# Output accumulators as two PSUM tiles, and the last unit in halves, in a convolution and rational-activation kernel

## The chip, the cores and the metric

The kernel runs on one core of one Trainium2 chip. The metric is the device time of one execution in microseconds (us), which is that of its one core. A core has five engines with a queue each: TensorE (PE in the profile; PEld is its weight load), VectorE (DVE), ScalarE (ACT), GpSimd (POOL) and SyncE (SP, which here only issues DMAs). Matmuls write to PSUM; ScalarE and VectorE read it.

## The reference, cut to what matters

```python
def _attn_ref(x, weight):                       # x (8, 4096, 192), weight (8, 7)
    w = softmax(weight, axis=-1)                # exp(weight - max) / (sum + 1e-9)
    x_pad = concatenate([zeros((B, 6, D)), x], axis=1)
    x_unf = x_pad[:, arange(S)[:, None] + arange(7)[None, :], :].reshape(B, S, 7, 8, 24)
    return einsum('hk,bskhg->bshg', w, x_unf).reshape(B, S, D)

def _moe_ref(x, w_in, w_out, a, b):             # x (32768, 192), w_in (192, 2048), w_out (2048, 192)
    h = x @ w_in
    P = a[0] + a[1]*h + a[2]*h**2 + a[3]*h**3
    Q = 1.0 + abs(b[0])*abs(h) + abs(b[1])*h**2
    g = P / (Q + 1e-6)
    return g @ w_out
```

A causal 7-tap convolution with softmaxed taps goes into two matrix products with a rational function between them.

## The kernel before, in words

The 32768 tokens are cut into 64 chunks of 512 (`NCH`, `CH`), and the 2048 hidden features into 8 units of 256 (`UPC`), so there are 512 units (`NU`); unit k is feature block k mod 8 of chunk k div 8. For each unit:

- TensorE makes the first product into a PSUM tile `hp` of 128 x 1024 (`gemm1`, line 512, ten matmuls, task `g1`); two such tiles exist.
- ScalarE makes five passes over 128 x 1024: `A` (line 583) and `S` into tile `t` (line 579), both from `hp`; `B` in place on `A` (line 586); `L`, a logarithm, into `l` (line 593); `Y`, an exponential, into a PSUM tile `y` (line 597).
- VectorE makes four passes, all recorded at the helper `stt` (line 305): `V` (`t<-t,hp`), `m` (`g<-t,y`), `e` (`A<-A,y`) and `g` (`g<-A,g`), the last of which finishes the unit.
- TensorE makes the second product (`gemm2`, line 521, task `g2`): eight matmuls add the unit to the chunk's output accumulator `op`, first the four of token pair 0, then the four of pair 1. The trace shows two PE records for each of these matmuls, so 16 for a unit.

The accumulator is one PSUM tile of 4 x 256 columns, from a pool with one buffer (`ps_o`). After a chunk's eighth unit ScalarE copies it out in two parts (`out_evac`, line 530, tasks `("O", c, 0)` and `("O", c, 1)`, tile `ob`), and SyncE sends each part to memory. The next chunk's accumulator takes the same buffer.

GpSimd and its accumulating DMAs do the convolution of a later chunk (tile `acc`), paced by VectorE's `g` passes.

The order on each engine is written out by a planner (`plan`): each task has an engine, an assumed cost, dependencies and a rank, and a simulated clock puts them into a list. The TensorE order is fixed by hand: `g1` of unit k, then `g2` of unit k-3 (`LAG`). `plan` already treats the two parts of the output separately: the first `g2` of a chunk depends, for pair p, on `("O", c - 1, p)` alone. The waits that the chip obeys, however, come from the tiles that the recorded instructions read and write.

The kernel has two bodies for two kinds of coefficients; the inputs here take the one called `fast`.

Of the kernel before, what the change touches and what calls it, by code (L numbers as in the profile page):

```python
# [10 lines left out]
F32 = mybir.dt.float32  # L11
# [5 lines left out]
ALU = mybir.AluOpType  # L17
# [3 lines left out]
NB, S, D = 8, 4096, 192  # L21
# [3 lines left out]
P = 128  # L25
CH = 512
NCH = T // CH
CPB = S // CH
FT = DF // P
UPC = FT // 2  # L30
NU = NCH * UPC
# [6 lines left out]
C_Q = 1.0 + EPS_Q  # L38
F64_MIN = float(np.uint32(0x38000000).view(np.float32))
LAG = 3  # L40
NG_BUF = LAG + 3
# [24 lines left out]
def plan(fast):  # L66
# [3 lines left out]
    def add(name, engine, cost, deps, rank, release=0):  # L70
        locked = (engine == "POOL" and name[0] != "a") or (engine == "DVE" and name[0] in LOCKED)
        tasks[name] = (engine, cost, [d for d in deps if d], rank, release, locked)
# [23 lines left out]
    pe = [("c", 0, 1), ("c", 0, 0)]  # L96
# [6 lines left out]
    for c in range(NCH):  # L103
        for k in range(KT if c > 1 else 0):
            rank = 8 * window(c, k)
            add(("x", c, k), "POOL", COST["x"], [after_unit(c, k), ("a", c, k - NTMP) if k > NTMP else None,
                ("x", c, k - 1) if k else ("x", c - 1, KT - 1) if c > 2 else ("t", 2)]
                + ([("l", c - 2, 1)] if k == 0 and c > 3 else []), rank)
            if k:
                add(("a", c, k), "POOL", COST["a"], [("x", c, k), ("a", c, k - 1) if k > 1 else ("x", c, 0)], rank)  # L110
        if c > 1:
            old = [("g1", (c - 2) * UPC + UPC - 1)]
            add(("h", c), "POOL", COST["h"], [("a", c, KT - 1), after_unit(c, KT + 2)] + old, -100)
        for half in range(2):
            if c > 1:
                add(("l", c, half), "POOL", COST["l"], [("h", c), ("l", c, 0) if half else None, after_unit(c, KT + 3 + half)], -100)
                continue
            rank = -48 - 8 * half + 8 * c * SECOND
            add(("xh", c, half), "ACT", COST["xh"] * (1 + 0.4 * half), [("c", c, half)], rank)
            add(("xl", c, half), "DVE", COST["xl"] * (1 + 0.4 * half), [("xh", c, half)], rank)  # L120
        for pair in range(2):
            add(("O", c, pair), "ACT", COST["O"], [("g2", c * UPC + UPC - 1, pair)],
                8 * ((c + 1) * UPC) + (19 if pair else -30))
    if not fast:
        add(("k", 0), "DVE", COST["k"], [], -50, BODY_AT)
# [1 line left out]
    for k in range(NU):  # L127
        c, i = divmod(k, UPC)

        def old(n, *names):  # L130
            return [(name, k - n) for name in names] if k >= n else []

        add(("g1", k), "PE", COST["g1"], [("l" if c > 1 else "xl", c, 0), ("l" if c > 1 else "xl", c, 1)] + old(2, "V", "A", "S")
            + ([wdep("i", i)] if c == 0 else []), 0)
        add(("S", k), "ACT", COST["S"], [("g1", k), ("kr", 0)] + old(4, "m"), 8 * k + 1)
        add(("A", k), "ACT", COST["A"], [("g1", k), ("kr", 0)] + old(4, "g"), 8 * k)
        if fast:
            add(("B", k), "ACT", COST["B"], [("A", k)], 8 * k + 0.5)
            add(("V", k), "DVE", COST["V"], [("S", k)], 8 * k + 2)
            add(("L", k), "ACT", COST["L"], [("B", k)] + old(2, "Y"), 8 * k + 3)  # L140
        else:
            add(("B", k), "ACT", COST["B"], [("g1", k), ("kr", 0)] + old(2, "Y"), 8 * k + 2)
            add(("Q", k), "POOL", COST["Q"], [("A", k), ("B", k)], 8 * k + 3)
            add(("U", k), "DVE", COST["U"], [("S", k)], 8 * k + 1)
            add(("V", k), "DVE", COST["V"], [("U", k)], 8 * k + 2)
            add(("L", k), "ACT", COST["L"], [("Q", k)], 8 * k + 3)
        add(("Y", k), "ACT", COST["Y"], [("L", k)] + old(1, "e")
            + ([("xl", 1, 0), ("xl", 1, 1)] if k == SECOND else []), 8 * k + 4)
        add(("m", k), "DVE", COST["m"], [("V", k), ("Y", k)] + old(NG_BUF, "G"), 8 * k + 5)
        add(("e", k), "DVE", COST["e"], [("Y", k)], 8 * k + 6)  # L150
        add(("g", k), "DVE", COST["g"], [("m", k), ("e", k)], 8 * k + 7)
        for pair in range(2):
            add(("g2", k, pair), "PE", COST["g2"], [("g", k)] + ([wdep("o", i)] if c == 0 else [])
                + ([("O", c - 1, pair)] if c and i == 0 else []), 0)
    for k in range(NU + LAG):
        if k == SECOND + SECOND_LAG:
            pe += [("c", 1, 1), ("c", 1, 0)]
        if k < NU:
            pe.append(("g1", k))
        if k >= LAG:  # L160
            pe += [("g2", k - LAG, 0), ("g2", k - LAG, 1)]

    after, need, ready = {}, {}, {}
# [41 lines left out]
def kernel(  # L205
# [13 lines left out]
    nc = tc.nc  # L219
# [84 lines left out]
    def stt(out_, a, s, b, op0, op1):  # L304
        return nc.vector.scalar_tensor_tensor(out=out_, in0=a, scalar=s, in1=b, op0=op0, op1=op1)  # L305
# [71 lines left out]
    def body(fast):  # L377
# [133 lines left out]
                for n, (w, part, x) in enumerate(terms):  # L511
                    nc.tensor.matmul(H[k][:, j, :], lhsT=w[:, i, part, j, :], rhs=x, start=(n == 0), stop=(n == 4))  # L512

        def gemm2(k, pair):
            c, i = divmod(k, UPC)
            if i == 0 and pair == 0:
                O[c] = ps_o.tile([P, 4, 256], F32, name="op")
            for j in range(2):
                f = 2 * i + j
                for t in (2 * pair, 2 * pair + 1):  # L520
                    nc.tensor.matmul(O[c][:, t, 0:D], lhsT=G[k][:, j, t * P:t * P + P], rhs=wo_t[:, f, :],  # L521
                                     start=(f == 0 and t % 2 == 0), stop=(f == FT - 1 and t % 2 == 1))
            if pair == 1:
                del G[k]

        def out_evac(c, pair):
            ob = opool.tile([P, 2, D], F32, name="ob")
            o = O[c][:, 2 * pair:2 * pair + 2, 0:D]
            if fast:
                nc.scalar.activation(out=ob, in_=o, func=AF.Copy, scale=K["rO"])  # L530
            else:
                nc.scalar.copy(out=ob, in_=o)
            nc.sync.dma_start(out=out_v[c, pair], in_=ob)
            if pair == 1:
                del O[c]

        def flat(t):
            return t.rearrange("p a b -> p (a b)")
# [28 lines left out]
                K["r" + name] = nc.scalar.alloc_register(f"r_{name}_{fast}")  # L567
                nc.scalar.reg_load(K["r" + name], x[0:1].bitcast(I32))

        def unit(kind, k):  # L570
            h = flat(H[k]) if k in H else None
            s = st.get(k, {})
            if kind == "k":
                coefficients()
            elif kind == "kr":
                registers()
            elif kind == "S":
                if fast:
                    nc.scalar.activation(out=work_tile(k, "t"), in_=h, func=AF.Square, scale=K["rt"], bias=1.0)  # L579
                else:  # L580
                    nc.scalar.activation(out=work_tile(k, "t"), in_=h, func=AF.Identity, scale=K["rt"], bias=K["c2"])
            elif kind == "A":
                nc.scalar.activation(out=work_tile(k, "A"), in_=h, func=AF.Abs, scale=K["rA"])  # L583
            elif kind == "B":
                if fast:
                    nc.scalar.activation(out=s["A"], in_=s["A"], func=AF.Square, bias=1.0)  # L586
                else:
                    nc.scalar.activation(out=work_tile(k, "l"), in_=h, func=AF.Square, scale=K["rB"])
            elif kind == "Q":
                nc.gpsimd.tensor_tensor(out=s["A"], in0=s["A"], in1=s["l"], op=ALU.add)  # L590
            elif kind == "L":
                if fast:
                    nc.scalar.activation(out=work_tile(k, "l"), in_=s["A"], func=AF.Ln, scale=K["rL"], bias=1.0)  # L593
                else:
                    nc.scalar.activation(out=s["l"], in_=s["A"], func=AF.Ln, bias=C_Q)
            elif kind == "Y":
                nc.scalar.activation(out=work_tile(k, "y"), in_=s["l"], func=AF.Exp, scale=-1.0)  # L597
            elif kind == "U":
                nc.vector.tensor_tensor(out=s["t"], in0=s["t"], in1=h, op=ALU.mult)
            elif kind == "V":  # L600
                stt(s["t"], s["t"], K["c1"], h, ALU.add, ALU.mult)
            elif kind == "m":
                G[k] = gpool.tile([P, 2, CH], F32, name="g")
                stt(flat(G[k]), s["t"], K["c0"], s["y"], ALU.add, ALU.mult)
            elif kind == "e":
                stt(s["A"], s["A"], K["d"] if fast else C_Q, s["y"], ALU.add, ALU.mult)
            elif kind == "g":
                last_step[k] = stt(flat(G[k]), s["A"], K["d2"] if fast else 2.0, flat(G[k]), ALU.subtract, ALU.mult).ins
                del st[k], H[k]

        with tc.manual_schedule(engines={E.PE, E.Activation, E.DVE, E.Pool}):
            for kind, *which in plan(fast):
# [67 lines left out]
```

## Time and profile before

| what | value |
|---|---|
| median of 3 runs | 2666.54 us (2665.88 to 2666.84) |
| the profiled execution | 2666.89 us |
| its span in the trace | 2664.70 us, so 2.19 us lie outside |
| mean granted TensorE clock | 0.995 of full speed |
| busy share of PE, DVE, ACT, POOL | 95%, 94%, 95%, 46% |

A row of the timeline gives start and duration in us, engine, line, operation and tiles; in brackets stands the idle time before it and what ended it. Durations overlap: an engine may start the next instruction before the one before has ended, so the pace is read from the distance of starts. In the waits, each row says which group waited for which, with the total in us, the count and the longest.

### The profile page before, as it was taken

To read this page: it belongs to the slowest core of one execution; us is meant where nothing else is said; L and a number is where in the kernel's file an instruction comes from. 1 tells how busy PE (TensorE), PEld (TensorE's weight loads), DVE (VectorE), ACT (ScalarE), POOL (GpSimd) and SP (SyncE) were. 2 spreads that over 40 slices of the span, in tenths; PEclk is the share of its full clock that TensorE was granted. 3 is DMA by queue.
4 is the path that set the end of the run, shared out by engine and by line. 5 is a ranking of instruction groups with operands and counts; after the bars stand their busy time and mean duration, and the time that the engine had idled before them with its cause. 6 is when DMAs were issued, how large, how long until landed. Compare 5 with 4: busy or idle time off the path is not lost.

```text
span 2664.7 us, 35994 instructions
## 1 busy us (share of the span) xinstructions
PE 2534.2 (95%) x13528; PEld 2299.1 (86%) x13528; DVE 2516.9 (94%) x2160; ACT 2539.2 (95%) x2739; POOL 1235.7 (46%) x1452
## 2 busy tenths in 40 slices
PE   5999999999999999999999999999999999999998
PEld 4888888888888888888888888888888888888887
DVE  8999999999999999999999999999999999999998
ACT  7999999999999999999999999999999999999997
POOL 4454454544544444545445445454454444454530
PEclk8999999999999999999999999999999999999999
DMA  5445444445444444444544544444444444444430
GB/s 156 99 98 107 101 100 99 97 104 104 92 105 101 99 103 102 98 105 93 107 96 97 107 102 99 99 97 103 104 94 104 102 98 103 102 98 104 94 76 14
DMA packets 101721, 263.96 MB, mean 99 GB/s; under 512 B 9760, under 2 KB 44832, under 8 KB 101536
## 3 DMA queue, kind: packets, MB, share of 16 engines
q0 software_dynamic: 53568, 195.06, 38.4%
q1 hardware_dynamic: 47664, 66.04, 8.5%
q8 instruction: 108, 1.77, 0.3%
q14 instruction: 77, 0.63, 0.1%
q10 hardware_dynamic: 304, 0.46, 0.1%
HBM read 41.32 MB, written 25.17 MB: 25 GB/s over the span
## 4 chain that ended last, share of the span: by engine, by line
PE 87%; ACT 8%; DVE 2%; issue 2%; DMA 0%; POOL 0%; SPq 0%; DVEq 0%; ACTq 0%
PE op L521 50%; PE hp L512 38%; ACT l L593 2%; ACT A L586 2%; ACT ob L530 2%; ACT t L579 1%; DVE g L305 1%; DVE A L305 0%; DVE t L305 0%; ACT y L597 0%; DVE wo_t L399 0%; ACT ad L385 0%; ACT A L583 0%; PE y L434 0%; DMA wb_t<-in_wband 0%
## 5 line engine op out<-in xcount | busy, mean ns | idle before, releaser
L521 PE MATMUL op<-wo_t,g 128*128 128x192 f32 x8192 | 1424.4, 327 | 100.9 <-ACT ob L530 90.3
L521 PEld LDWEIGHTS op<-wo_t,g 128*128 128x128 f32 x8192 | 1355.6, 190 | 163.8 <-ACT ob L530 116.4
L512 PE MATMUL hp<-xh,wh_t 128*128 128x512 f32 x2048 | 872.5, 426 | 15.3 <-DVE t L305 10.6
L305 DVE SCALAR_TENSOR_TENSOR g<-t,cf,y 128x1024 f32<-128x1024 f32 x512 | 655.2, 1280 | 95.6 <-ACT y L597 78.9
L305 DVE SCALAR_TENSOR_TENSOR t<-t,cf,hp 128x1024 f32<-128x1024 f32 x512 | 653.9, 1277 | 33.8 <-ACT t L579 33.8
L305 DVE SCALAR_TENSOR_TENSOR g<-A,cf,g 128x1024 f32<-128x1024 f32 x512 | 657.0, 1283 | 1.2
L305 DVE SCALAR_TENSOR_TENSOR A<-A,cf,y 128x1024 f32<-128x1024 f32 x512 | 654.0, 1277 | 0.0
L512 PE MATMUL hp<-xh,wl_t 128*128 128x512 f32 x2048 | 633.5, 391 | 0.0
L583 ACT ACTIVATE A<-hp 128x1024 f32<-128x1024 f32 x512 | 522.1, 1020 | 49.5 <-PE hp L512 33.3
L593 ACT ACTIVATE l<-A 128x1024 f32<-128x1024 f32 x512 | 542.6, 1060 | 6.2
L586 ACT ACTIVATE A<-A 128x1024 f32<-128x1024 f32 x512 | 541.6, 1058 | 0.0
L597 ACT ACTIVATE y<-l 128x1024 f32<-128x1024 f32 x512 | 525.6, 1027 | 4.2 <-DVE xl L499 0.2
L579 ACT ACTIVATE t<-hp 128x1024 f32<-128x1024 f32 x512 | 522.0, 1020 | 0.0
L447 POOL TENSOR_SCALAR tmp<-xt,wt_t,zero 128x512 f32<-128x512 f32 x496 | 377.5, 767 | 209.3 <-DVE g L305 202.6
L512 PEld LDWEIGHTS hp<-xh,wl_t 128*128 128x128 f32 x2048 | 386.1, 189 | 86.7 <-DVE wl_t L407 0.2
L512 PEld LDWEIGHTS hp<-xh,wh_t 128*128 128x128 f32 x2048 | 387.1, 189 | 80.0 <-DVE t L305 7.3
L453 POOL DMA_DIRECT2D acc<-tmp x248 | 214.9, 867 | 414.0 <-DMA acc<-xs 369.1
L512 PE MATMUL hp<-xl,wh_t 128*128 128x512 f32 x1024 | 403.4, 394 | 0.0
L447 POOL TENSOR_SCALAR xs<-xt,wt_t,zero 128x512 f32<-128x512 f32 x248 | 188.7, 767 | 205.8 <-DVE g L305 205.8
L512 PEld LDWEIGHTS hp<-xl,wh_t 128*128 128x128 f32 x1024 | 194.2, 190 | 20.4 <-DVE xl L499 0.3
L473 POOL TENSOR_SCALAR xh<-acc,one,zero 128x1024 fp32r<-128x1024 f32 x62 | 74.2, 1198 | 251.0 <-DVE g L305 245.6
L453 POOL DMA_DIRECT2D acc<-xs x124 | 109.4, 882 | 61.3 <-DMA acc<-tmp 43.1
(57 smaller groups left out, 424.3 us busy)
## 6 DMA issues: line engine op xcount, KB each, us to landing
acc<-tmp POOLq DMA_DIRECT2D x248, 512.0 KB, 4.5
acc<-xs POOLq DMA_DIRECT2D x124, 512.0 KB, 5.2
xt<-in_xt SPq DMA_DIRECT2D x62, 518.0 KB, 4.0
out<-ob SPq DMA_DIRECT2D x128, 192.0 KB, 2.6
raw<-in_w_in SPq DMA_DIRECT2D x8, 512.0 KB, 5.7
raw<-in_w_out SPq DMA_DIRECT2D x8, 384.0 KB, 4.1
xs<-in_xa ACTq DMA_DIRECT2D x1, 324.0 KB, 4.7
xs<-in_xa SPq DMA_DIRECT2D x1, 324.0 KB, 6.5
```

The costliest lines, as they stand in the source:

```text
L305: return nc.vector.scalar_tensor_tensor(out=out_, in0=a, scalar=s, in1=b, op0=op0, op1=op1)
L447: ins = nc.gpsimd.tensor_scalar(to[:, n * CH:n * CH + CH], of[:, n * XA + k:n * XA + k + CH], wt_t[:, n, k:k + 1], zero, ALU.mult, ALU.add)
L453: nc.gpsimd.dma_start(out=CP[c], in_=TMP.pop((c, k)), accum_op=ALU.add)
L473: ins = nc.gpsimd.tensor_scalar(X[c][0].rearrange("p a b -> p (a b)"), CP[c], one, zero, ALU.mult, ALU.add)
L512: nc.tensor.matmul(H[k][:, j, :], lhsT=w[:, i, part, j, :], rhs=x, start=(n == 0), stop=(n == 4))
L521: nc.tensor.matmul(O[c][:, t, 0:D], lhsT=G[k][:, j, t * P:t * P + P], rhs=wo_t[:, f, :], start=(f == 0 and t % 2 == 0), stop=(f == FT - 1 ...
L530: nc.scalar.activation(out=ob, in_=o, func=AF.Copy, scale=K["rO"])
L579: nc.scalar.activation(out=work_tile(k, "t"), in_=h, func=AF.Square, scale=K["rt"], bias=1.0)
L583: nc.scalar.activation(out=work_tile(k, "A"), in_=h, func=AF.Abs, scale=K["rA"])
L586: nc.scalar.activation(out=s["A"], in_=s["A"], func=AF.Square, bias=1.0)
L593: nc.scalar.activation(out=work_tile(k, "l"), in_=s["A"], func=AF.Ln, scale=K["rL"], bias=1.0)
L597: nc.scalar.activation(out=work_tile(k, "y"), in_=s["l"], func=AF.Exp, scale=-1.0)
```

## The change

The accumulator becomes two tiles, `op0` and `op1`, of 2 x 256 columns each, one for each token pair, each with a buffer of its own; `gemm2` allocates the pair's tile when its chunk begins, and `out_evac` reads the pair's tile and drops it. In the last unit (k = 511) the passes `m`, `e` and `g` run on halves of 512 columns each, with half-size matmul groups behind each half, and the last chunk's output copies depend on the second half.

```diff
@@ -119,7 +119,7 @@
             add(("xh", c, half), "ACT", COST["xh"] * (1 + 0.4 * half), [("c", c, half)], rank)
             add(("xl", c, half), "DVE", COST["xl"] * (1 + 0.4 * half), [("xh", c, half)], rank)
         for pair in range(2):
-            add(("O", c, pair), "ACT", COST["O"], [("g2", c * UPC + UPC - 1, pair)],
+            add(("O", c, pair), "ACT", COST["O"], [("g2", c * UPC + UPC - 1, pair) + ((1,) if c == NCH - 1 else ())],
                 8 * ((c + 1) * UPC) + (19 if pair else -30))
     if not fast:
         add(("k", 0), "DVE", COST["k"], [], -50, BODY_AT)
@@ -146,6 +146,14 @@
             add(("L", k), "ACT", COST["L"], [("Q", k)], 8 * k + 3)
         add(("Y", k), "ACT", COST["Y"], [("L", k)] + old(1, "e")
             + ([("xl", 1, 0), ("xl", 1, 1)] if k == SECOND else []), 8 * k + 4)
+        if k == NU - 1:
+            for j in range(2):
+                add(("m", k, j), "DVE", 670, [("V", k), ("Y", k)] + old(NG_BUF, "G"), 8 * k + 4 * j)
+                add(("e", k, j), "DVE", 670, [("Y", k)], 8 * k + 4 * j + 1)
+                add(("g", k, j), "DVE", 670, [("m", k, j), ("e", k, j)], 8 * k + 4 * j + 2)
+                for pair in range(2):
+                    add(("g2", k, pair, j), "PE", COST["g2"] / 2, [("g", k, j)], 0)
+            continue
         add(("m", k), "DVE", COST["m"], [("V", k), ("Y", k)] + old(NG_BUF, "G"), 8 * k + 5)
         add(("e", k), "DVE", COST["e"], [("Y", k)], 8 * k + 6)
         add(("g", k), "DVE", COST["g"], [("m", k), ("e", k)], 8 * k + 7)
@@ -157,7 +165,9 @@
             pe += [("c", 1, 1), ("c", 1, 0)]
         if k < NU:
             pe.append(("g1", k))
-        if k >= LAG:
+        if k == NU + LAG - 1:
+            pe += [("g2", k - LAG, pair, j) for j in range(2) for pair in range(2)]
+        elif k >= LAG:
             pe += [("g2", k - LAG, 0), ("g2", k - LAG, 1)]
 
     after, need, ready = {}, {}, {}
@@ -511,28 +521,26 @@
                 for n, (w, part, x) in enumerate(terms):
                     nc.tensor.matmul(H[k][:, j, :], lhsT=w[:, i, part, j, :], rhs=x, start=(n == 0), stop=(n == 4))
 
-        def gemm2(k, pair):
+        def gemm2(k, pair, only=None):
             c, i = divmod(k, UPC)
-            if i == 0 and pair == 0:
-                O[c] = ps_o.tile([P, 4, 256], F32, name="op")
-            for j in range(2):
+            if i == 0:
+                O[c, pair] = ps_o.tile([P, 2, 256], F32, name=f"op{pair}")
+            for j in range(2) if only is None else [only]:
                 f = 2 * i + j
                 for t in (2 * pair, 2 * pair + 1):
-                    nc.tensor.matmul(O[c][:, t, 0:D], lhsT=G[k][:, j, t * P:t * P + P], rhs=wo_t[:, f, :],
+                    nc.tensor.matmul(O[c, pair][:, t % 2, 0:D], lhsT=G[k][:, j, t * P:t * P + P], rhs=wo_t[:, f, :],
                                      start=(f == 0 and t % 2 == 0), stop=(f == FT - 1 and t % 2 == 1))
-            if pair == 1:
+            if pair == 1 and only != 0:
                 del G[k]
 
         def out_evac(c, pair):
             ob = opool.tile([P, 2, D], F32, name="ob")
-            o = O[c][:, 2 * pair:2 * pair + 2, 0:D]
+            o = O.pop((c, pair))[:, :, 0:D]
             if fast:
                 nc.scalar.activation(out=ob, in_=o, func=AF.Copy, scale=K["rO"])
             else:
                 nc.scalar.copy(out=ob, in_=o)
             nc.sync.dma_start(out=out_v[c, pair], in_=ob)
-            if pair == 1:
-                del O[c]
 
         def flat(t):
             return t.rearrange("p a b -> p (a b)")
@@ -567,8 +575,9 @@
                 K["r" + name] = nc.scalar.alloc_register(f"r_{name}_{fast}")
                 nc.scalar.reg_load(K["r" + name], x[0:1].bitcast(I32))
 
-        def unit(kind, k):
+        def unit(kind, k, *half):
             h = flat(H[k]) if k in H else None
+            part = slice(CH * half[0], CH * half[0] + CH) if half else slice(0, W)
             s = st.get(k, {})
             if kind == "k":
                 coefficients()
@@ -600,13 +609,16 @@
             elif kind == "V":
                 stt(s["t"], s["t"], K["c1"], h, ALU.add, ALU.mult)
             elif kind == "m":
-                G[k] = gpool.tile([P, 2, CH], F32, name="g")
-                stt(flat(G[k]), s["t"], K["c0"], s["y"], ALU.add, ALU.mult)
+                if half in ((), (0,)):
+                    G[k] = gpool.tile([P, 2, CH], F32, name="g")
+                stt(flat(G[k])[:, part], s["t"][:, part], K["c0"], s["y"][:, part], ALU.add, ALU.mult)
             elif kind == "e":
-                stt(s["A"], s["A"], K["d"] if fast else C_Q, s["y"], ALU.add, ALU.mult)
+                stt(s["A"][:, part], s["A"][:, part], K["d"] if fast else C_Q, s["y"][:, part], ALU.add, ALU.mult)
             elif kind == "g":
-                last_step[k] = stt(flat(G[k]), s["A"], K["d2"] if fast else 2.0, flat(G[k]), ALU.subtract, ALU.mult).ins
-                del st[k], H[k]
+                g = flat(G[k])[:, part]
+                last_step[k] = stt(g, s["A"][:, part], K["d2"] if fast else 2.0, g, ALU.subtract, ALU.mult).ins
+                if half != (0,):
+                    del st[k], H[k]
 
         with tc.manual_schedule(engines={E.PE, E.Activation, E.DVE, E.Pool}):
             for kind, *which in plan(fast):
```

On all engines the instructions stand in the order of before, except in the last unit; what differs elsewhere is which tile is named and which waits are set. On TensorE at a chunk boundary in the middle of the kernel, before: the last first-product matmuls of a unit and then the new chunk's first second-product matmuls (in brackets the engines waited for; 49 is the number of the fast body's semaphores).

```order
L512 MATMUL hp_13357<-xl_13096,wh_t_182 128x512
L512 MATMUL hp_13357<-xh_13095,wh_t_182 128x512
L512 MATMUL hp_13357<-xh_13095,wl_t_183 128x512 x2
L521 MATMUL op_13374<-wo_t_184,g_13315 128x192 [waits DVE_49,PE_49,Activation_49]
L521 MATMUL op_13374<-wo_t_184,g_13315 128x192 x7
L512 MATMUL hp_13396<-xh_13095,wh_t_182 128x512 [waits DVE_49]
```

The same place on TensorE in the changed kernel:

```order
L522 MATMUL hp_13400<-xl_13139,wh_t_182 128x512
L522 MATMUL hp_13400<-xh_13138,wh_t_182 128x512
L522 MATMUL hp_13400<-xh_13138,wl_t_183 128x512 x2
L531 MATMUL op0_13417<-wo_t_184,g_13358 128x192 [waits DVE_49,Activation_49]
L531 MATMUL op0_13417<-wo_t_184,g_13358 128x192 x3
L531 MATMUL op1_13428<-wo_t_184,g_13358 128x192 [waits Activation_49]
L531 MATMUL op1_13428<-wo_t_184,g_13358 128x192 x3
L522 MATMUL hp_13440<-xh_13138,wh_t_182 128x512 [waits DVE_49]
```

The one wait for ScalarE ahead of eight matmuls has become one ahead of the first four and another ahead of the last four. On ScalarE at the same boundary, before (`ob<-op` is the output copy; the DMAHW wait is for an old transfer out of the buffer `ob`):

```order
L597 ACTIVATE y_13341<-l_13330 128x1024 [waits DVE_49,Activation_49]
L530 ACTIVATE ob_13347<-op_13076 128x384 [waits DMAHW6_49,PE_49]
L586 ACTIVATE A_13337<-A_13337 128x1024 [waits Activation_49]
L579 ACTIVATE t_13368<-hp_13317 128x1024
L593 ACTIVATE l_13371<-A_13337 128x1024 [waits Activation_49]
L530 ACTIVATE ob_13379<-op_13076 128x384 [waits DMAHW7_49]
L597 ACTIVATE y_13382<-l_13371 128x1024 [waits DVE_49,Activation_49]
```

The same place on ScalarE in the changed kernel:

```order
L606 ACTIVATE y_13384<-l_13373 128x1024 [waits DVE_49,Activation_49]
L540 ACTIVATE ob_13390<-op0_13118 128x384 [waits DMAHW6_49,PE_49]
L595 ACTIVATE A_13380<-A_13380 128x1024 [waits Activation_49]
L588 ACTIVATE t_13411<-hp_13360 128x1024
L602 ACTIVATE l_13414<-A_13380 128x1024 [waits Activation_49]
L540 ACTIVATE ob_13422<-op1_13129 128x384 [waits DMAHW7_49,PE_49]
L606 ACTIVATE y_13425<-l_13414 128x1024 [waits DVE_49,Activation_49]
```

No pass has moved; the second copy has a wait of its own for TensorE, and the first names only the pair's tile. On VectorE at the end of the kernel, the last seven passes of before are the last unit but one's `V` and `g` among them, and then `m`, `e`, `g` of the last unit:

```order
L305 SCALAR_TENSOR_TENSOR t_19456<-t_19456,cf_117,hp_19426 128x1024 [waits PE_49,Activation_49]
L305 SCALAR_TENSOR_TENSOR g_19458<-A_19414,cf_117,g_19458 128x1024 [waits DVE_49]
L305 SCALAR_TENSOR_TENSOR g_19476<-t_19456,cf_117,y_19473 128x1024 [waits DVE_49,Activation_49]
L305 SCALAR_TENSOR_TENSOR A_19450<-A_19450,cf_117,y_19473 128x1024
L305 SCALAR_TENSOR_TENSOR g_19476<-A_19450,cf_117,g_19476 128x1024 [waits DVE_49]
```

In the changed kernel VectorE ends so:

```order
L315 SCALAR_TENSOR_TENSOR t_19520<-t_19520,cf_117,hp_19490 128x1024 [waits PE_49,Activation_49]
L315 SCALAR_TENSOR_TENSOR g_19522<-A_19478,cf_117,g_19522 128x1024 [waits DVE_49]
L315 SCALAR_TENSOR_TENSOR g_19540<-t_19520,cf_117,y_19537 128x512 [waits DVE_49,Activation_49]
L315 SCALAR_TENSOR_TENSOR A_19514<-A_19514,cf_117,y_19537 128x512
L315 SCALAR_TENSOR_TENSOR g_19540<-t_19520,cf_117,y_19537 128x512
L315 SCALAR_TENSOR_TENSOR g_19540<-A_19514,cf_117,g_19540 128x512 [waits DVE_49]
L315 SCALAR_TENSOR_TENSOR A_19514<-A_19514,cf_117,y_19537 128x512
L315 SCALAR_TENSOR_TENSOR g_19540<-A_19514,cf_117,g_19540 128x512 [waits DVE_49]
```

Three passes have become six, in the order m, e of half 0, m of half 1, g of half 0, e and g of half 1; TensorE's last eight matmuls become two groups of four, one for each half, with a wait for VectorE ahead of each.

## Rows read from the trace of the kernel before

**Rows 1.** Part 1 of the page: busy time, share of span, instructions of each engine

```profile
PE 2534.2 (95%) x13528; PEld 2299.1 (86%) x13528; DVE 2516.9 (94%) x2160; ACT 2539.2 (95%) x2739; POOL 1235.7 (46%) x1452
```

**Rows 2.** The waits, whole span: us in total, times, longest

```profile
PE op L521 <- ACT ob L530: 90.3, 62, 2.4
...
ACT ob L530 <- PE op L521: 49.6, 64, 7.5
```

**Rows 3.** Timeline of PE ahead of a chunk boundary and at it

```profile
1756.70 2.76 PE L521 MATMUL op<-wo_t,g 128*128 128x192 f32 x16
...
1761.58 2.76 PE L521 MATMUL op<-wo_t,g 128*128 128x192 f32 x16
...
1764.04 0.53 PE L512 MATMUL hp<-xh,wh_t 128*128 128x512 f32 x1
...
1768.10 2.87 PE L521 MATMUL op<-wo_t,g 128*128 128x192 f32 x16 [1.48 <-ACT ob L530]
```

**Rows 4.** Timeline of ACT around the same boundary

```profile
1762.70 1.02 ACT L597 ACTIVATE y<-l 128x1024 f32<-128x1024 f32 x1
1764.38 0.49 ACT L530 ACTIVATE ob<-op 128x384 f32<-128x384 f32 x1 [0.66 <-PE op L521]
...
1767.56 0.49 ACT L530 ACTIVATE ob<-op 128x384 f32<-128x384 f32 x1
1767.93 1.04 ACT L597 ACTIVATE y<-l 128x1024 f32<-128x1024 f32 x1
...
1770.68 1.08 ACT L586 ACTIVATE A<-A 128x1024 f32<-128x1024 f32 x1
1771.80 1.06 ACT L593 ACTIVATE l<-A 128x1024 f32<-128x1024 f32 x1
```

**Rows 5.** Timeline of PE, line 521: first matmuls of chunks 1, 5, 7, 63

```profile
94.67 0.65 PE L521 MATMUL op<-wo_t,g 128*128 128x192 f32 x3
...
256.01 4.55 PE L521 MATMUL op<-wo_t,g 128*128 128x192 f32 x16 [2.43 <-ACT ob L530]
...
339.34 0.92 PE L521 MATMUL op<-wo_t,g 128*128 128x192 f32 x4 [1.48 <-ACT ob L530]
...
2625.37 2.87 PE L521 MATMUL op<-wo_t,g 128*128 128x192 f32 x16 [1.48 <-ACT ob L530]
```

**Rows 6.** Windows: busy time by engine, then granted clock (PEclk), DMA share, GB/s

```profile
258.50:260.30 1.80, 1.80 (x8) 1.80 (x7) 1.80 (x3) 1.80 (x3) 1.55 (x2) 0.52 0.00 0
1768.10:1773.10 5.00, 5.00 (x26) 4.58 (x27) 5.00 (x5) 4.73 (x5) 3.40 (x4) 1.00 0.14 43
1768.10:1808.93 40.83, 39.34 (x209) 35.74 (x209) 38.72 (x33) 39.30 (x43) 19.52 (x23) 1.00 0.49 101
```

**Rows 7.** Timeline of DVE, PE and ACT at the end of the kernel

```profile
2651.87 1.28 DVE L305 SCALAR_TENSOR_TENSOR g<-t,cf,y 128x1024 f32<-128x1024 f32 x1
...
2652.01 2.87 PE L521 MATMUL op<-wo_t,g 128*128 128x192 f32 x16 [1.62 <-DVE g L305]
2653.06 1.28 DVE L305 SCALAR_TENSOR_TENSOR A<-A,cf,y 128x1024 f32<-128x1024 f32 x1
2654.38 1.28 DVE L305 SCALAR_TENSOR_TENSOR g<-A,cf,g 128x1024 f32<-128x1024 f32 x1
...
2655.72 2.87 PE L521 MATMUL op<-wo_t,g 128*128 128x192 f32 x16 [0.84 <-DVE g L305]
2658.62 0.87 ACT L530 ACTIVATE ob<-op 128x384 f32<-128x384 f32 x2 [7.49 <-PE op L521]
```

**Rows 8.** Timeline of DVE, two passes of 512 columns in the preparation (`y` in PSUM)

```profile
13.83 0.69 DVE L499 TENSOR_TENSOR xl<-y,xh 128x512 fp32r<-128x512 f32 x1
14.44 0.68 DVE L407 TENSOR_TENSOR wl_t<-tr,wh_t 128x512 fp32r<-128x512 f32 x1
```

**Rows 9.** Timeline of POOL at the next boundary

```profile
1803.18 0.85 POOL L453 DMA_DIRECT2D acc<-tmp  x1 [5.76 <-DMA acc<-xs]
...
1810.22 1.20 POOL L473 TENSOR_SCALAR xh<-acc,one,zero 128x1024 fp32r<-128x1024 f32 x1 [4.15 <-DVE g L305]
```

## The prediction

> **What bounds the kernel now.** I read the busy shares first, then the waits, then the timeline of the engine that the waits point at. The busy shares [rows 1] decide nothing: PE, DVE and ACT are all at 94 or 95%, so any of them may be the pace once another is relieved. The waits [rows 2] show one wait of size on PE: 62 times, 90.3 us in all, the second products (`op`, line 521) wait for ScalarE's output copy (`ob`, line 530). ScalarE in turn waits 64 times, 49.6 us, for PE ahead of such a copy. The timeline shows the place. Ahead of a chunk boundary PE runs without a gap: a second product starts at 1756.70 and the next at 1761.58, so a unit takes 4.88 us, and eight take 39.04; of this the second product has 1764.04 - 1761.58 = 2.46 and the first product 2.42 [rows 3]. The new chunk's first second product would be due at 1764.04 + 2.42 = 1766.46; it starts at 1768.10, released by `ob` [rows 3]. On ScalarE the first copy starts at 1764.38, after 0.66 us of idle, 0.34 us after PE has gone on from all sixteen records of the last unit (1764.04): it waits for both pairs. The second copy stands behind three more passes, starts at 1767.56, takes 0.49 and so ends at 1768.05, just ahead of PE's start [rows 4]. PE therefore waits for the second copy though its next four matmuls overwrite only what the first copy has read.
>
> From chunk 7 (339.34) to chunk 63 (2625.37) [rows 5] there are 56 periods in 2286.03 us, 40.82 each, equal to the window of one chunk [rows 6]. That is 1.78 over the dense 39.04: 1.64 of lateness (1768.10 - 1766.46), and the other 0.14 by subtraction in the first unit after the gap. So the boundary costs 1.78 per chunk on the engine that sets the end, and nothing else in the period does.
>
> **The change part by part.** *Two tiles, the first copy.* Pair 0's four matmuls go out by 1761.58 + 1.23 = 1762.81; with the same 0.34 us of tail the copy may start at 1763.15. ScalarE is free of `y` 0.93 us after 1762.70 (the pace of a pass, worked out below), at 1763.63 [rows 4]. So the copy starts at 1763.63 instead of 1764.38, and all behind it on ScalarE comes 0.75 us earlier.
>
> *Two tiles, the first second product.* It now needs only the first copy, which ends at 1763.63 + 0.49 = 1764.12, over 2 us ahead of 1766.46: no wait. Pair 1's four matmuls are due at 1766.46 + 1.23 = 1767.69. The second copy ends at 1768.05 - 0.75 = 1767.30. It is in time by 0.39 us. Queued behind this new wait on PE are the next first product and all after it; if the copy were late, PE would be late by the same amount. The extra wait itself, when satisfied, I cost at nothing: every second product already has one for DVE, and the unit at 1761.58 shows no gap from it.
>
> *What is late next.* VectorE's 32 passes and ScalarE's passes must fit into 39.04 us. ScalarE from 1764.38 to 1771.80 waits for nothing: two copies and seven passes in 7.42 us [rows 4]. A copy takes 0.37 (1767.56 to 1767.93); a pass that needs the one directly before it takes 1771.80 - 1770.68 = 1.12 instead of its plain pace. So the other six take (7.42 - 0.74 - 1.12) / 6 = 0.93 each. A chunk has 40 passes, two copies, and, counted in ScalarE's order, five passes that follow directly on the one they need: 35 x 0.93 + 5 x 1.12 + 0.74 = 38.9 us. That is under 39.04, by only 0.1 to 0.2. VectorE is busy 38.72 in a chunk with the gap in it [rows 6]. So PE is the next bound, at 39.04, with ScalarE close behind.
>
> *GpSimd.* Its taps are paced by `g` passes and its accumulating DMAs. The last such DMA of a chunk issues at 1803.18; the step that reads its sum (`xh`) starts 7.04 us later, released by `g` after 4.15 idle, and the wait of 5.76 ahead of that DMA shows how long one may take to land [rows 9]. With the boundary 1.78 shorter 5.26 are left, so `xh` may be late by some 0.5. I cost it at nothing: by the code `xh` follows the second unit of a chunk and is first needed by the next chunk's first product, seven units on. Without that cover it would be 62 x 0.5 = 31 us.
>
> *The early chunks.* From chunk 1 (94.67) to chunk 7 (339.34) there are 244.67 us [rows 5] against 6 x 39.04 = 234.24: 10.4 us over. [...] ScalarE's order changes over in these chunks, so I leave 1 us and take 9.4 (both ends: 8 to 10.4).
>
> *The last unit in halves.* Count from `m` at 2651.87 [rows 7]. Now: `m`, `e`, `g` end at 2654.38 + 1.28 = +3.79, PE starts at +3.85, the first copy at +6.75 (2658.62), the second a copy's 0.4 later, +7.14. For a pass of half the columns the nearest row is 13.83 to 14.44: 0.61 to the next start, 0.69 to its end [rows 8], against 1.19 (2651.87 to 2653.06) for a whole one. Six halves start at 0, 0.61, 1.22, 1.83, 2.44 and, because the last needs the one before it (0.04 after its end, as 2654.38 is after 2653.06 + 1.28), 3.17; the last ends at +3.86, 0.07 later than now. Half 0 is finished at 1.83 + 0.69 = +2.52; PE is then still in the unit before (2652.01, so until about +2.7), takes half 0's matmuls (1.23) to +3.93, and half 1's to 5.16, both without a gap. The second copy starts 0.34 later, +5.5: 1.6 us earlier than now. Both ends: 0.6 (each half costs 0.1 us more, and PE stands 0.4 between its groups) and 1.8 (the halves at exactly half of 1.19, and half 1 no later than now). I take 1.6, since the row of 512 columns is at hand.
>
> [...]
>
> **The sum.** 56 x 1.78 = 99.7, early chunks 9.4, end 1.6: 110.7 us. 2666.89 (the profiled execution; 2664.70 span and 2.19 outside, which stays) - 110.7 = 2556.2. The median of the runs shown is 2666.54, 0.35 lower, so 2556 it is.
>
> **The rivals.** *ScalarE becomes the pace.* For: its busy time in a chunk is 39.30 us [rows 6], more than 39.04, and my 38.9 is only 0.1 below. Against: those 39.30 contain the long ends of passes that wait for one another, while an engine that is free starts the next before the last ends. If 39.30 is the floor, each of the 62 chunks costs 0.26 more: 16 us, 2572.
>
> *The wait moves to pair 1.* If the first copy gains nothing (ScalarE held up by something that idle hid), the second still ends at 1768.05, 0.36 us after 1767.69, and PE stands there instead, with the 0.14 behind a gap: 62 x 0.5 = 31 us more, 2587. For: the second copy has not moved in ScalarE's order. Against: the 0.66 us of idle ahead of the first copy has PE as its releaser, in 64 cases [rows 2].
>
> *The change does nothing at the boundaries.* If the waits were for the whole buffer as before, only the end gains: 2665. Against: the first copy and the first matmuls now name different tiles, and the instruction order shows two waits.
>
> *Slower: the clock falls in the middle of the second product.* The new wait stands inside a run of matmuls. If the second copy came so late that PE stood there as long as at 256.01, the clock would fall at each boundary as it did there. That gap is 0.95 longer than 1.48, and the sixteen records took 1.68 longer: 2.6 us a chunk over now, 62 x 2.6 = 163, 2830. It decides from a gap longer than 1.48, for those leave the clock at 1.00 [rows 6]; the second copy would have to end 1.1 us after its present 1768.05. Nothing in ScalarE's order does that.
>
> **How the numbers follow.** The forecast, 2556 (2552 to 2564), has 68%; ScalarE as the pace 16% (2564 to 2580, the point 2572); the wait moved to pair 1 9% (2580 to 2600); nothing at the boundaries 4%; slower 3%. About 0.2% (5 us) is what a measurement of this kernel can tell from no change. The low end, 2550, is the sum with the early chunks and the end at their upper bounds (10.4, 1.8: 2555), less 5, because 4.88 is read to 0.01 us and there are 496 units from chunk 1 to 62; the high end is 2582, which takes in ScalarE as the pace and the start of the next rival, and leaves out some 15%. Faster are the first three, 93%; the gain at the end alone is within 0.2%, so the fourth is the 4% for the same; slower 3%.
>
> **What would show it.** Right: the wait of `op` for `ob` on PE falls from 90.3 us to a few; ScalarE's idle ahead of the first copy is gone; the period of a chunk in mid-kernel is 39.04; no second product takes over 4 us after a gap at a boundary; the end from the last `m` to the second copy is about 5.5 us. Wrong: a period of 39.3 with PE waiting for `g` or first products waiting for `t` and `A` (ScalarE is the pace); a gap of PE before pair 1's matmuls (the wait has moved); a period of 40.8 (nothing changed).

## The result and the profile after

The changed kernel takes 2556.32 us (median of 4 runs, 2555.94 to 2556.80) against 2666.61 before: a ratio of 0.9587, 95% interval 0.957 to 0.9604. Run again later, it took 2556.58 against 2666.09, ratio 0.9588 (0.9571 to 0.9605). The profiled execution took 2555.94, its span 2554.0: 110.7 us less than the span of before.

Part 1 of the page after, which answers to [rows 1]:

```profile
PE 2514.7 (98%) x13528; PEld 2303.2 (90%) x13528; DVE 2495.3 (98%) x2163; ACT 2513.6 (98%) x2739; POOL 1244.6 (49%) x1452
```

Busy times barely moved; the span closed around them. The waits after, whole span (us in total, times, longest), which answer to [rows 2]:

```profile
DVE g L315 <- ACT y L606: 35.3, 58, 0.6
...
PE op L531 <- DVE g L315: 10.0, 3, 6.4
...
ACT ob L540 <- PE op L531: 7.8, 2, 7.6
```

PE has no row any more of `op` waiting for `ob` (90.3 us before). ScalarE's 49.6 us ahead of its copies are 7.8, and those at the end of the kernel.

PE at a chunk boundary after, which answers to [rows 3]:

```profile
1689.92 2.76 PE L531 MATMUL op<-wo_t,g 128*128 128x192 f32 x16
1694.80 2.76 PE L531 MATMUL op<-wo_t,g 128*128 128x192 f32 x16
1699.68 2.76 PE L531 MATMUL op<-wo_t,g 128*128 128x192 f32 x16
```

The second row is the new chunk's first second product. It starts 4.88 us after the one before it, like any other. ScalarE at this boundary, which answers to [rows 4]:

```profile
1691.04 1.02 ACT L606 ACTIVATE y<-l 128x1024 f32<-128x1024 f32 x1
1691.99 0.48 ACT L540 ACTIVATE ob<-op 128x384 f32<-128x384 f32 x1
...
1695.16 0.50 ACT L540 ACTIVATE ob<-op 128x384 f32<-128x384 f32 x1
```

The first copy starts 2.07 us after the last unit's second product (1689.92), with no idle ahead of it; the prediction had 1763.63 - 1761.58 = 2.05. The second copy ends at 1695.66, and pair 1's matmuls are due at 1694.80 + 1.23 = 1696.03: in time by 0.37 us, where 0.39 was forecast. The chunk's window, in the columns of [rows 6]:

```profile
1694.80:1733.84 39.04, 39.04 (x209) 35.82 (x208) 38.35 (x33) 38.86 (x43) 19.63 (x23) 1.00 0.51 106
```

PE is busy for all of the 39.04 us, at full clock. Between 800 and 2400 us the first copies of 41 chunks lie 39.04 us apart in every case (39 chunks, 40.82 on average, before).

The end of the kernel after, first VectorE and PE, then the second copy; it answers to [rows 7]:

```profile
2541.27 0.74 DVE L315 SCALAR_TENSOR_TENSOR g<-t,cf,y 128x512 f32<-128x512 f32 x1
2541.41 7.15 PE L531 MATMUL op<-wo_t,g 128*128 128x192 f32 x32 [1.88 <-DVE g L315]
2541.92 0.74 DVE L315 SCALAR_TENSOR_TENSOR A<-A,cf,y 128x512 f32<-128x512 f32 x1
...
2544.68 0.75 DVE L315 SCALAR_TENSOR_TENSOR g<-A,cf,g 128x512 f32<-128x512 f32 x1
...
2548.59 0.49 ACT L540 ACTIVATE ob<-op 128x384 f32<-128x384 f32 x1 [0.16 <-PE op L531]
```

From the last unit's first `m` to the second copy there are 7.32 us, where before there were 7.14 (2651.87 to 2659.01) and 5.5 were forecast. The last 32 records took 7.15, and a window within them shows why:

```profile
2543.50:2546.00 2.50, 2.50 (x9) 2.50 (x9) 1.90 (x3) 0.00 (x0) 0.00 (x0) 0.50 0.01 3
```

The granted clock was 0.50 there. PE had stood for 1.88 us ahead of the last unit but one's second product, and was within it when the clock fell: 1.00 from 2542.00 to 2542.50, 0.74 in the half microsecond after.

### The profile page after: what moved, and what is told of

Read it like the earlier page. It is cut to its first block, busy times and chain, and to the rows that moved or that the text cites. A ratio compares the mean times of both kernels' runs of the same rounds, so it can differ in the third digit from the quotient of the medians.

```text
span 2554.0 us, 36060 instructions
## 1 busy us (share of the span) xinstructions
PE 2514.7 (98%) x13528; PEld 2303.2 (90%) x13528; DVE 2495.3 (98%) x2163; ACT 2513.6 (98%) x2739; POOL 1244.6 (49%) x1452
## 4 chain that ended last, share of the span: by engine, by line
ACT 57%; DVE 20%; issue 14%; PE 9%; DMA 0%; DVEq 0%; ACTq 0%; SPq 0%
ACT y L606 14%; ACT A L595 12%; ACT t L588 10%; ACT l L602 10%; ACT A L592 9%; DVE A L315 7%; DVE t L315 7%; DVE g L315 6%; PE op L531 5%; PE hp L522 4%; ACT ob L540 2%; ACT ad L395 0%; ACT ad L397 0%; PE y L444 0%; DVE wo_t L409 0%
## 5 line engine op out<-in xcount | busy, mean ns | idle before, releaser
L457 POOL TENSOR_SCALAR tmp<-xt,wt_t,zero 128x512 f32<-128x512 f32 x496 | 383.5, 787 | 191.8 <-DVE g L315 185.2
```

The lines of the kernel that those rows point to most:

```text
L457: ins = nc.gpsimd.tensor_scalar(to[:, n * CH:n * CH + CH], of[:, n * XA + k:n * XA + k + CH], wt_t[:, n, k:k + 1], zero, ALU.mult, ALU.add)
```

## The experiments

Four questions were open: which part of the change gives the 110 us, and by which of the two waits; how much room ScalarE has at 39.04; what happened at the end; and how long half a VectorE pass takes. The edits are against the changed kernel where nothing else is said, and are cut to the lines that matter.

**Each part alone.** With the tiles alone, the last unit runs whole, and its second product and the last output copies are planned like those of any other unit:

```diff
-        if k == NU - 1:
+        if False:
```

> Two accumulator tiles, last unit whole. Theory (all of the gain is at the chunk boundaries; the halves at the end gave nothing because the granted clock fell there): PE period per chunk 39.04 us as with both parts, time 2556 to 2559. At the end PE again stands some 1.9 us ahead of unit 510's second product, so the clock falls here too; from the last unit's first VectorE pass m to the second copy 8 to 10 us (7.32 with both parts, 7.14 before). Rival (the halves cost by themselves, by more instructions and waits): without them that end takes 7.1 us or less and the time is 2556.1 or less. Rival (part of the 110 us came from the end): 2560 or more.

Measured: 2556.97 us (2556.54 to 2558.47), ratio 0.9591 (0.9575 to 0.9607), period 39.04. So the tiles give all of the 110 us that can be told by the time. The end:

```profile
2542.51 1.28 DVE L313 SCALAR_TENSOR_TENSOR g<-t,cf,y 128x1024 f32<-128x1024 f32 x1
2542.65 2.87 PE L529 MATMUL op<-wo_t,g 128*128 128x192 f32 x16 [1.87 <-DVE g L313]
...
2546.36 2.87 PE L529 MATMUL op<-wo_t,g 128*128 128x192 f32 x16 [0.84 <-DVE g L313]
...
2549.26 0.49 ACT L538 ACTIVATE ob<-op 128x384 f32<-128x384 f32 x1 [0.81 <-PE op L529]
```

Here 8 to 10 us were expected, and that was a miss: behind the same gap, 1.87 us, the sixteen records take 2.87, the clock was 1.00 from 2540.80 to 2549.30, and the end takes 6.75 us. That is 0.39 less than before: the first copy no longer waits for both pairs, so only the second is left behind the last matmul.

With the halves alone, the accumulator is one tile again:

```diff
-            if i == 0:
-                O[c, pair] = ps_o.tile([P, 2, 256], F32, name=f"op{pair}")
+            if i == 0 and pair == 0:
+                O[c] = ps_o.tile([P, 4, 256], F32, name="op")
```

> One accumulator tile as before, last unit in halves. Theory (boundary waits untouched; ahead of unit 510 PE stands 1.62 us as before and the clock stays at 1.00): period 40.82 us, wait of op for ob on PE near 90 us, and from the last m to the second copy 5.7 to 6.0 us instead of 7.14, time 2665.4 (2665 to 2666). Rival (the halves themselves cost): that end takes 7.3 us and the time is 2666.6 to 2667.

Measured: 2665.54 us (2663.79 to 2666.55), ratio 0.9997 (0.9988 to 1.0007), which the time does not tell from no change. The wait is there as before:

```profile
PE op L531 <- ACT ob L540: 90.4, 62, 2.4
```

and the end, in the timeline:

```profile
2649.84 0.74 DVE L315 SCALAR_TENSOR_TENSOR g<-t,cf,y 128x512 f32<-128x512 f32 x1
2649.98 5.65 PE L531 MATMUL op<-wo_t,g 128*128 128x192 f32 x32 [1.62 <-DVE g L315]
...
2655.66 0.87 ACT L540 ACTIVATE ob<-op 128x384 f32<-128x384 f32 x2 [6.56 <-PE op L531]
```

The second copy starts 0.39 after the first, at 2656.05 (the pace of a copy, 0.87 - 0.48 for the two in this row): 6.21 us after `m`, 0.93 less than before. The expectation said 5.7 to 6.0; right in direction, somewhat short in size.

This trace shows one thing more, which bears on the early chunks. Ahead of the same chunk PE stands for 2.43 us, as in the kernel before at 256.01 [rows 5], and the slow records do not follow:

```profile
256.91 2.87 PE L531 MATMUL op<-wo_t,g 128*128 128x192 f32 x16 [2.43 <-ACT ob L540]
```

The sixteen records take 2.87 us, as at the end of the kernel before where the clock is 1.00 (2652.01 to 2654.88), instead of 4.55; and from chunk 1 to chunk 7 there are 242.91 us (95.63 to 338.53) instead of 244.67.

**Which wait it was.** Two kernels take one of the two waits away and leave the other. In the first, the kernel before gets its second copy earlier on ScalarE, and keeps the single tile:

```diff
-                8 * ((c + 1) * UPC) + (19 if pair else -30))
+                8 * ((c + 1) * UPC) + (-29.9 if pair else -30))
```

> The kernel before (one tile, whole last unit), with the second copy planned directly behind the first on ScalarE (rank -29.9 instead of 19); the planner puts one pass between them. Theory (PE's gap is the late second copy; ScalarE's wait for all sixteen matmuls is a second, smaller loss): the second copy ends well ahead of the next first second-product, PE's wait for ob falls to near nothing, ScalarE keeps an idle of up to 0.7 us per chunk and has little room for it: period 39.1 to 39.5, time 2562 to 2590. Rival (the single tile itself serializes, whatever the order): period 40.8, time 2666. Rival (ScalarE has ample room): 39.04, time 2558.

Measured: 2572.80 us (2571.09 to 2573.18), ratio 0.9649 (0.9633 to 0.9666), period 39.24. PE's wait for `ob` is gone without a second tile. What is left is on ScalarE:

```profile
1741.16 0.49 ACT L530 ACTIVATE ob<-op 128x384 f32<-128x384 f32 x1 [0.18 <-PE op L521]
1741.54 1.06 ACT L586 ACTIVATE A<-A 128x1024 f32<-128x1024 f32 x1
1742.49 0.48 ACT L530 ACTIVATE ob<-op 128x384 f32<-128x384 f32 x1
```

and in the waits of this kernel:

```profile
ACT ob L530 <- PE op L521: 29.4, 63, 8.4
```

The first copy still waits for all sixteen records, 0.18 us at this boundary and 0.43 at the one before, and ScalarE has little to give: 0.20 us per chunk over 39.04.

In the second, the changed kernel needs the second copy at once, because pair 1 goes first in the first unit of a chunk:

```diff
-            pe += [("g2", k - LAG, 0), ("g2", k - LAG, 1)]
+            pe += [("g2", k - LAG, p) for p in ((1, 0) if k > LAG and (k - LAG) % UPC == 0 else (0, 1))]
```

> The changed kernel, but in the first unit of each chunk pair 1's four matmuls go ahead of pair 0's, so that PE needs the second copy at once and only the earlier release of the first copy (0.66 us of ScalarE idle) is kept. Theory: the second copy ends some 0.75 us earlier than before but PE needs it at the start: a gap of 0.7 to 0.9 us and some 0.14 to 0.3 behind it, period 40.0 to 40.2, time 2615 to 2630. Rival (the first copy's earlier release alone gives it all): 39.04, 2556. Rival (it gives nothing alone): 40.8, 2666.

Measured: 2611.44 us (2609.86 to 2611.53), ratio 0.9794 (0.9778 to 0.981), period 40.00; the time is just under the range expected, the period at its edge. PE at a boundary:

```profile
1724.45 2.76 PE L531 MATMUL op<-wo_t,g 128*128 128x192 f32 x16
1730.17 2.87 PE L531 MATMUL op<-wo_t,g 128*128 128x192 f32 x16 [0.68 <-ACT ob L540]
```

The new chunk starts 5.72 us after the unit before instead of 4.88: 0.84 late. So the period falls from 40.82 to 40.00 by the first copy's release, and from 40.00 to 39.04 because pair 0's matmuls do not need the second copy: 0.82 and 0.96 of the 1.78.

**How much room ScalarE has.** One and two more ScalarE copies per chunk, of scratch data, in mid-chunk (`range(2)` in the second kernel):

```diff
                 nc.scalar.activation(out=work_tile(k, "A"), in_=h, func=AF.Abs, scale=K["rA"])
+                if k % UPC == 4:
+                    for _ in range(1):
+                        nc.scalar.copy(out=idle_out, in_=idle_in)
```

> The changed kernel with one more ScalarE copy of 128 x 384 per chunk (scratch to scratch, some 0.38 us), in mid-chunk. It measures how much room ScalarE has. Theory (38.8 to 38.9 us of work against PE's 39.04): the copy uses up the room and 0.1 to 0.25 us per chunk come on top: period 39.15 to 39.3, time 2563 to 2572. Rival (ScalarE was already the pace): 39.4, 2580. Rival (ample room): 39.04, 2556.

> The same with two such copies per chunk. Theory: once ScalarE is the pace, the second copy counts in full: 0.38 us per chunk and 24 us more than with one: 39.5 to 39.7, time 2587 to 2596. Rival (ample room): 2556 to 2565. The line through one and two copies gives the room by where it meets 39.04.

Measured: 2568.43 us (2567.10 to 2569.22), ratio 0.9634 (0.9617 to 0.9651), period 39.23; and 2602.15 (2601.39 to 2603.13), ratio 0.976 (0.9742 to 0.9777), period 39.77. What one copy adds on ScalarE, start to start:

```profile
1709.75 0.50 ACT L598 COPY idle_out<-idle_in 128x384 f32<-128x384 f32 x1
1710.15 1.03 ACT L612 ACTIVATE y<-l 128x1024 f32<-128x1024 f32 x1
```

That is 0.40, and with two of them 0.95:

```profile
1732.68 1.05 ACT L598 COPY idle_out<-idle_in 128x384 f32<-128x384 f32 x2
1733.63 1.02 ACT L612 ACTIVATE y<-l 128x1024 f32<-128x1024 f32 x1
```

A period of 39.23 less 0.40 is 38.83, and 39.77 less 0.95 is 38.82. Both kernels agree: ScalarE's own work in a chunk is 38.82 us, and its room against PE is 0.22. The first run was as the theory had it; the second came out higher than its range, because two copies in a row cost 0.95 and not 0.76. Where ScalarE is the pace, PE feels it as another rival of the prediction: it waits for the second copy ahead of pair 1. With one copy it is the weight load that waits, and the waits (total, count, longest) come to 11.6 us over 62 boundaries, 0.19 each, the whole of 39.23 - 39.04:

```profile
PEld op L534 <- ACT ob L543: 11.6, 56, 1.1
```

With two copies PE's timeline shows it:

```profile
1725.45 1.46 PE L534 MATMUL op<-wo_t,g 128*128 128x192 f32 x8
1727.09 1.57 PE L534 MATMUL op<-wo_t,g 128*128 128x192 f32 x8 [0.18 <-ACT ob L543]
```

The chunk's first second product falls apart into two groups of eight records: PE stands ahead of pair 1 until the second copy is done.

**The end.** The changed kernel once more:

> The changed kernel once more, for the end alone. In its first trace the granted clock fell to 0.50 within the last two second products, behind a gap of 1.88 us; with the two tiles alone the same gap of 1.87 left it at full speed. Theory (whether the clock falls behind a gap of that length differs from one execution to the next): here it may stay, and then from the last m to the second copy 5.9 to 6.2 us. Rival (it falls whenever the halves follow that gap): 7.3 us again.

```profile
2542.93 0.74 DVE L315 SCALAR_TENSOR_TENSOR g<-t,cf,y 128x512 f32<-128x512 f32 x1
2543.07 5.65 PE L531 MATMUL op<-wo_t,g 128*128 128x192 f32 x32 [1.88 <-DVE g L315]
...
2548.76 0.49 ACT L540 ACTIVATE ob<-op 128x384 f32<-128x384 f32 x1 [0.16 <-PE op L531]
```

Behind the same gap of 1.88 us the clock stayed at full speed, 1.00 from 2540.00 to 2548.70: 5.65 us for 32 records, and 5.83 from `m` to the second copy. The rival, that it always falls, is out.

With eight unused matmuls in that gap:

```diff
+            if k == NU - 2 and pair == 0:
+                spare = ps_h.tile([P, 2, CH], F32, name="hp")
+                for j in range(2):
+                    for n in range(4):
+                        nc.tensor.matmul(spare[:, j, :], lhsT=wh_t[:, n, 0, j, :], rhs=X[c][1], start=(n == 0), stop=(n == 3))
```

> The changed kernel with eight matmuls of 512 columns, whose result is not used, on PE ahead of unit 510's second product, where PE stands 1.88 us. Theory (the end loses to the clock that falls in or behind that gap): no gap over 0.5 us, clock 1.00 to the end, the last 32 records of op in 5.4 to 5.7 us instead of 7.15, from the last m to the second copy 5.8 to 6.2 us, time 2555 to 2556. Rival (the halves' own chain of passes sets the end): 7.3 us and 2556.3.

```profile
2542.53 0.74 DVE L315 SCALAR_TENSOR_TENSOR g<-t,cf,y 128x512 f32<-128x512 f32 x1
2542.67 5.65 PE L536 MATMUL op<-wo_t,g 128*128 128x192 f32 x32
...
2548.36 0.49 ACT L545 ACTIVATE ob<-op 128x384 f32<-128x384 f32 x1 [0.16 <-PE op L536]
```

Measured: 2555.79 us (2555.12 to 2556.18), ratio 0.9585 (0.9568 to 0.9602). The clock was 1.00 from 2540.00 to 2548.30, and the end takes 5.83 us, as without these matmuls where the clock stays; the ranges of the two kernels' times overlap, so that this version is faster is not shown. The other traces say more of that gap than these two of the changed kernel. Ahead of the last unit but one's second product PE stands 1.87 us with the tiles alone and 1.88 in the changed kernel once more, and the clock stays at 1.00. It falls to 0.50 behind 1.88 us in the first trace of the changed kernel; and behind 1.90 us with the early second copy the last 32 records take the same 7.15 us:

```profile
2555.30 7.15 PE L521 MATMUL op<-wo_t,g 128*128 128x192 f32 x32 [1.90 <-DVE g L305]
```

With one and with two more ScalarE copies the longest wait of ScalarE for PE ahead of an output copy is 6.1 us, as in the changed kernel once more (7.6 in its first trace), which speaks for a clock that stays there too. What decides between the two is open.

Last, the length of half a pass. The coefficients that VectorE's passes read from columns of `cf` become constants, so that the rational function is another one:

```diff
-        K = {"c0": col(40), "c1": col(41), "d": col(32), "d2": col(42)} if fast else {}
+        K = {"c0": 0.5, "c1": 0.25, "d": 0.125, "d2": 2.0} if fast else {}
```

> The changed kernel with constants in place of the computed coefficients as the scalar operand of VectorE's four passes (so the rational function is another one). It measures a VectorE pass by itself: the prediction took 0.61 us from start to start for half a pass, from a row whose operation has no column of coefficients as an operand, and it was 0.66. Theory (an operand that is a column in memory costs some 0.06 us per instruction): half passes 0.60, whole passes 1.13 instead of 1.19; the time stays at 2556, since PE sets the pace. Rival (the 0.05 belong to the second source or to PSUM): 0.66 and 1.19 as before.

```profile
2537.05 1.22 DVE L315 SCALAR_TENSOR_TENSOR g<-A,g 128x1024 f32<-128x1024 f32 x1
2538.18 0.68 DVE L315 SCALAR_TENSOR_TENSOR g<-t,y 128x512 f32<-128x512 f32 x1
2538.32 5.47 PE L531 MATMUL op<-wo_t,g 128*128 128x192 f32 x32 [1.17 <-DVE g L315]
2538.78 0.68 DVE L315 SCALAR_TENSOR_TENSOR A<-A,y 128x512 f32<-128x512 f32 x1
...
2541.29 0.69 DVE L315 SCALAR_TENSOR_TENSOR g<-A,g 128x512 f32<-128x512 f32 x1
2543.82 0.49 ACT L540 ACTIVATE ob<-op 128x384 f32<-128x384 f32 x1 [0.16 <-PE op L531]
```

A whole pass goes from 1.19 to 1.13 us, start to start, and a half from 0.66 to 0.60: 0.06 for each instruction at both lengths. The passes read the same tiles as before, so the rival (the second source or PSUM) is out. The period is 39.04 like the changed kernel's though VectorE's 32 passes of a chunk are 1.9 us shorter: VectorE is not the pace. The one time, 2551.27, lies 5 us lower, where no change was expected. Against the first trace of the changed kernel, 2.1 us of it lie ahead of chunk 1's first second product (91.67 instead of 93.79), 2.4 between chunk 63's and the second copy (31.55 instead of 33.95, which holds the slow clock), and 0.3 between; why the start is shorter is open.

## Why the prediction was right

2556 was forecast and 2556.32 measured. Its likeliest case, PE dense at 39.04 us with ScalarE just behind, is what the trace shows. That the sum of 110.7 us fits to 0.1 is luck: the early chunks gave 0.6 more than their term and the end 1.9 less (counted from chunk 63), and 1.2 us ahead of chunk 1 and behind the last copy, for which the sum has no term, made up for the rest.

- *What bounds it.* The chain was right: one late copy on ScalarE, and a first copy that waits for both pairs. An earlier second copy alone, with one tile, gives 39.24; the first copy's earlier release alone gives 40.00; the whole change gives 39.04.
- *The boundary, 56 x 1.78 = 99.7.* Period 40.82 to 39.04, as forecast, and the two margins that were walked through by hand (the first copy's start, the second copy's 0.39 us in hand) came out to 0.02 us.
- *The early chunks, 9.4.* From the first second product of chunk 1 to that of chunk 63, [rows 5] have 2530.70 us, and the profile after 2420.85 (93.79 to 2514.64), against 62 x 39.04 = 2420.48. Only 0.4 us are left where 1 was allowed for: the term is 10.0. But some 1.7 of it (4.55 - 2.87) are the slow clock behind the gap of 2.43 (0.52 from 258.50 to 260.30 [rows 6]), which is no fixed part of the kernel before: the kernel with the halves alone has that gap with sixteen records in 2.87 us behind it and 242.91 us from chunk 1 to 7, against which the term would be 8.3. The rival that had the clock fall at each boundary where PE stood that long took for certain what happened in one of two traces.
- *ScalarE's room.* Forecast 38.9 us of work in a chunk, measured 38.82. The rival that took its busy time of 39.30 for a floor fell: the window after has 38.86 busy and no wait of PE on it. How narrow it was is real, though: one copy of 0.40 more and ScalarE is the pace.
- *GpSimd.* It was put at nothing, rightly: in the profile after PE has no idle in the window of a chunk.
- *The end, 1.6: the step that failed in size.* It rested on 0.61 us for half a pass [rows 8], a row of an operation without a column of coefficients. The halves take 0.66, so that the last `g` ends at +4.16 (2544.68 + 0.75 - 2541.27) and not at +3.86. Where the clock stays the end takes 5.83 where 5.5 was forecast. The kernel with constants parts the two errors: its halves take 0.60 and its last `g` ends at +3.80 (2541.29 + 0.69 - 2538.18), yet its end takes 5.64. So the longer halves cost 0.19, and the other 0.14 is the walk of PE: its last 32 records run without a gap there and take 5.47, so that the copy starts 0.14 + 5.47 + 0.03 after `m`. Against the 7.14 of before 5.83 is a gain of 1.3 us instead of 1.6, of which 0.39 come with the tiles alone and 0.93 with the halves alone. In the first profiled execution the clock fell to 0.50 on top, for which the term had nothing, and the gain was -0.2. Half a pass of `g`, which has no source in PSUM, takes 0.66 (2543.24 to 2543.90), the same as one of `m`, which reads `y` there (2542.58 to 2543.24); with constants for the column both take 0.60 (2539.97 to 2540.57, 2539.37 to 2539.97).
- *What was not in the sum.* Chunk 1's first second product came at 93.79 instead of 94.67, 0.9 us earlier. The same program has it at 95.44 in its second trace, so this is the scatter of single executions. With the 0.3 us later start of the last copy counted from chunk 63 (33.95 instead of 33.64) and 0.3 less behind it, the parts add up: 0.9 + 109.85 - 0.3 + 0.3 = 110.7.

## What to carry to other kernels

Where a planner knows that two halves of a buffer are independent, look at whether the waits that the chip obeys know it too: the same order with one tile and with two differed by 1.78 us at every chunk boundary. When a bubble on the pacing engine is to go, walk the next engine's instructions through the new boundary one by one and add up its work per period, by distances of starts and not by busy time; here 0.22 us of room decided between 2556 and more. A loss that one trace shows once, like the slow clock behind a single gap, may be missing in the next execution, and a term that counts on it is a chance and not a gain. And a price for a half-size instruction should come from a row with the same kinds of operands.

## What the runs showed of the hardware that had not been expected

- A VectorE pass of this kernel with a column in memory as its scalar operand took 0.06 us more than with a constant, at 512 and at 1024 columns alike (0.66 against 0.60, 1.19 against 1.13).
- Behind gaps of nearly the same length PE kept its clock of 1.00 in two executions (1.87 us with the tiles alone, 1.88 in the changed kernel once more) and had slow records in two (1.88 in the first trace of the changed kernel, with 0.50 between 2543.50 and 2546.00, and 1.90 with the early second copy; 7.15 us for 32 records in both). Behind a gap of 2.43 sixteen records took 4.55 us in the kernel before (0.52 from 258.50 to 260.30) and 2.87 in the one with the halves alone. The gaps of 1.48 at the boundaries before left the clock at 1.00 (mean from 339.34 to 2625.37).
- Two equal copies of 128 x 384 in a row on ScalarE, writing the same tile, took 0.95 us together where one took 0.40. The last two output copies of the kernel with the halves alone, which write two buffers, start 0.39 apart.
